# First channel-mixing block in chunks of 1024 tokens, with products of 512 columns and four accumulator banks

## Chip, cores and metric

The kernel runs on one NeuronCore of a Trainium2 chip. The metric is the device time of one execution in microseconds (us); shorter is better.

## The reference

Three blocks follow one another, all in float32. A Fourier block (`rfft` along the sequence, a complex 256 x 256 product, a soft threshold, `irfft`) makes 4 x 3072 tokens of 256 features. The first channel-mixing block follows and is the place of the change; the second one ends the program:

```python
h = x @ w_in                    # 12288 x 256 by 256 x 2048
x = (h - np.tanh(h)) @ w_out    # 2048 x 256

xk = mu_k * x + (1.0 - mu_k) * x_prev
xr = mu_r * x + (1.0 - mu_r) * x_prev
k = np.maximum(xk @ w_k, 0.0)   # 256 x 1024
v = k * k @ w_v                 # 1024 x 256
out = sigmoid(xr @ w_r) * v
```

## The kernel before

Every float32 operand of a product is split in two parts of type float32r, `h` (a copy that rounds, on ScalarE) and `l` (the rest, subtracted on VectorE). One float32 product is then three matmuls, weights `h` by data `h`, `l` by `h` and `h` by `l`, accumulated in one bank of PSUM.

The program has three stages. Stage 1 is the Fourier block (to about 340 us in the profile), which leaves its tokens in DRAM (`ydr`). Stage 2 is the first channel-mixing block. It takes the tokens in 24 chunks of 512 (`chunks`, `CK` = 512). Stage 3, from about 1390 us, is the second block, in chunks of 512 too.

In stage 2, `reg_t` loads a chunk (`yr`) and `token_forms` makes seven forms of it, 256 columns each, for a fast 2 x 2 block product: three blocks of the chunk (B11, B21, B22) and four sums and differences (T1 to T4, made in `yt4`). They are converted to `yh` and `yl`; even chunks have theirs in the pool `pw`, odd chunks in `q1`, so that there are two sets. The weights `w_in` have seven such forms as well (`ah`, `al`).

`reg_pair(c, f2)` is one pass of a chunk over an eighth of the hidden features, and calls `reg_h`. That makes seven products of 256 columns (21 matmuls): one in a bank `g`, two one behind the other in a second bank `g`, and four one behind the other in a bank `m` (tag `y` or `a` in turn). Between two products in a bank its sum is read: from `g` by a copy on ScalarE (`copy`, L819), from `m` by an add on VectorE (`add`, L822), the last one by a copy on ScalarE (L847). Then come tanh (L862), the subtraction (L863), the split in `gh` and `gl` (L345, L348), and 12 matmuls of 512 columns with `w_out`, which add to two accumulator banks `v`. The accumulators are emptied after the eighth pass (L885, L886).

No engine's order is written by hand. Every operation is registered with a priority and an assumed duration, and `_Plan.run` lists the operations in the order in which they would start: of those whose inputs and tiles are free, an engine takes the one with the lowest priority number. On the chip each engine then works through its list in that order, and waits where the list says. A tile of a tag with n buffers can be made anew when all users of the tile n places before it are done.

Of the kernel before, what the change touches and what calls it, by code (L numbers as in the profile page):

```python
# [148 lines left out]
class _Plan:  # L149
# [6 lines left out]
    def op(self, eng, dur, emit, prio, writes=(), reads=(), after=(), lat=SEM, seq=True, nbytes=0):  # L156
# [6 lines left out]
        o.creates, o.frees = [], []  # L163
        for t in reads:
            deps.update(t.writers)
            t.readers.append(o)
        for t in writes:
# [9 lines left out]
            deps.update(r for r in t.readers if r is not o)  # L177
# [134 lines left out]
def fourier_moe_kernel(tc, x, w_r, w_i, b_r, b_i, w_in, w_out, mu_k, mu_r, w_k, w_v, w_rr, c_f, c_e, c_t, c_b, out, nb=B, ydump=None):  # L312
# [291 lines left out]
    def reg_conv(i):  # L604
# [23 lines left out]
        dma("pool" if i < EARLY else "sp", load, pr, [raw[0]], [], 524288, after=[qt[divmod(RAW0 + i * RAW1 // 4, NU)].writers[0] if i < EARLY else yload[int(K["l0"] + K["l1"] * (i - EARLY))]])  # L628
# [79 lines left out]
    def tt(o, a, b, alu, n, prio, writes, reads, **kw):  # L708
        op("dve", c_dve(n), lambda: dve.tensor_tensor(out=o(), in0=a(), in1=b(), op=alu), prio, writes, reads, **kw)
# [5 lines left out]

    def reg_weight(pool_, i, prio):
        st = stage(i, prio)
        h = tile_(pool_, [128, 512], F32R, f"wh{i}")
        l = tile_(pool_, [128, 512], F32R, f"wl{i}")
        hi(whole(h), whole(st), 512, prio)  # L720
        lo(whole(l), whole(st), whole(h), 512, prio)
        return h, l
# [39 lines left out]
    def token_forms(y, t, h, l, pr):
        def yb(d, k):
            return lambda: y()[:, d, k * HK:k * HK + HK]

        def tb(i):
            return lambda: t()[:, i]

        tt(tb(0), yb(0, 1), yb(0, 0), ALU.subtract, HK, pr, [t], [y])
        tt(tb(2), yb(1, 1), yb(0, 1), ALU.subtract, HK, pr, [t], [y], seq=False)  # L770
        tt(tb(1), yb(1, 1), tb(0), ALU.subtract, HK, pr, [t], [y])
        tt(tb(3), yb(1, 0), tb(1), ALU.subtract, HK, pr, [t], [y])
        for o, n, st, src in ((0, 1, y, lambda: y()[:, 0:1, 0:HK]), (1, 2, y, lambda: y()[:, 1].rearrange("p (k c) -> p k c", k=2)), (3, 4, t, t)):
            oc = lambda r, o=o, n=n: r[:, o:o + n]
            hi(cut(h[0], lambda r, oc=oc: oc(h[1](r))), (st, src), n * HK, pr)
            lo(cut(l[0], lambda r, oc=oc: oc(l[1](r))), (st, src), cut(h[0], lambda r, oc=oc: oc(h[1](r))), n * HK, pr)

    def same(r):
        return r

    def reg_t(c):
        b, j = chunks[c]
        pr = P2 + 8 * c - K["t"]
# [5 lines left out]
        c0 = j * CK  # L789
        deps = [ydr[b][k] for k in range(c0 // CH, (c0 + CK - 1) // CH + 1)]  # L790
        dma("sp", lambda: sp.dma_start(out=y(), in_=ydr_t[b][:, :, c0:c0 + CK]), pr - 8, [y], deps, 524288)
        yload.append(plan.ops[-1])

        token_forms(y, t, (h, same), (l, same), pr)
        tv[c] = (h, l)
# [4 lines left out]
    A11, A12, A22, S1, S2, S3, S4 = range(7)  # L800
    B11, B21, B22, T1, T2, T3, T4 = range(7)

    def reg_h(tokens, view, weights, ai, z0, tag):
        yh, yl = tokens
        ah, al = weights

        def product(o, a, t, prio, first):
            def e():
                w, wl_ = ah()[:, a, ai], al()[:, a, ai]
                v, vl = view[0](yh())[:, t], view[1](yl())[:, t]  # L810
                d = o()[:, 0:HK]
                mm(d, w, v, first, False, skip_group_check=True)
                mm(d, wl_, v, False, False, skip_group_check=True)
                mm(d, w, vl, False, True, skip_group_check=True)

            op("pe", 3 * 119, e, prio, [o], [ah, al, yh, yl])

        def copy(o, p, prio):
            op("act", c_act(HK, True), lambda: act.activation(out=o(), in_=p()[:, 0:HK], func=ACTF.Copy), prio, [o], [p])  # L819

        def add(t, half, p, s, prio):
            op("dve", c_dve(HK), lambda: dve.tensor_tensor(out=t()[:, half * HK:half * HK + HK], in0=p()[:, 0:HK], in1=s(), op=ALU.add), prio, [t], [p, s], seq=False)  # L822

        s2 = bank("g")
        p2 = tile_(q1, [128, HK], F32, "p2", 2)
# [3 lines left out]
        p5 = tile_(q1, [128, HK], F32, "p5", 2)  # L829
        p3 = tile_(q1, [128, HK], F32, "p3", 2)  # L830
# [5 lines left out]
        h0 = tile_(q1, [128, CK], F32, "hs0", 2)  # L836
        h1 = tile_(q1, [128, CK], F32, "hs1", 2)
        product(m, A11, B11, z0, True)
        add(h0, 0, m, p2, z0)
        product(m, S2, T2, z0, False)  # L840
        add(h0, 1, m, p3, z0)
        product(m, S3, T3, z0, False)
        add(h1, 1, m, p5, z0)
        product(m, A22, T4, z0, False)

        def last(func):
            op("act", c_act(HK, True), lambda: act.activation(out=h1()[:, 0:HK], in_=m()[:, 0:HK], func=func), z0, [h1], [m], seq=False)  # L847

        return h0, h1, m, last

    def reg_pair(c, f2):
        z0 = P2 + 8 * c + f2
        ai = f2 % 2

        h0, h1, m, last = reg_h(tv[c], (same, same), win[f2 // 2], ai, z0, 'ya'[f2 % 2] if c else 'y')
        last(ACTF.Copy)
        gg = []
        for hs in (h0, h1):
            th = tile_(q1, [128, CK], F32, "th", 2)
            gh = tile_(q1, [128, CK], F32R, "gh2", 3)  # L860
            gl = tile_(q1, [128, CK], F32R, "gl2", 3)
            op("act", c_act(CK, False), lambda th=th, hs=hs: act.activation(out=th(), in_=hs(), func=ACTF.Tanh), z0, [th], [hs])  # L862
            op("dve", c_dve(CK), lambda th=th, hs=hs: dve.tensor_tensor(out=hs(), in0=hs(), in1=th(), op=ALU.subtract), z0, [hs], [th])  # L863
            hi(whole(gh), whole(hs), CK, z0)
            lo(whole(gl), whole(hs), whole(gh), CK, z0)
# [5 lines left out]
        for k in range(2):  # L871
            gh, gl = gg[k]

            def e(k=k, gh=gh, gl=gl):
                for e_ in range(2):
                    s = slice(k * 256 + e_ * 128, k * 256 + e_ * 128 + 128)
                    mm(x2[e_](), wh_()[:, s], gh(), f2 == 0 and k == 0, False)
                    mm(x2[e_](), wl_()[:, s], gh(), False, False)
                    mm(x2[e_](), wh_()[:, s], gl(), False, f2 == 7 and k == 1)

            op("pe", 6 * 232, e, z0 + K["out"], x2, [gh, gl, wh_, wl_])
        if f2 == 7:
            b, j = chunks[c]
            t = tile_(q3, [128, 2, CK], F32, "x2", 2)
            op("act", c_act(CK, True), lambda: act.activation(out=t()[:, 0], in_=x2[0](), func=ACTF.Copy), z0 + K["x2"], [t], [x2[0]])  # L885
            op("act", c_act(CK, True), lambda: act.activation(out=t()[:, 1], in_=x2[1](), func=ACTF.Copy), z0 + K["x2"], [t], [x2[1]], seq=False)  # L886
            dma("sp", lambda: sp.dma_start(out=xdr_t[b][:, :, j * CK:j * CK + CK], in_=t()), z0 + K["x2"], [xdr[b, j]], [t], 524288)

    for c in range(len(chunks)):
# [3 lines left out]
    for c in range(len(chunks) - 1):  # L893
# [6 lines left out]
    wk = [reg_forms(q3, "k", 16, P3 - 30)]  # L900
    wt[24] = [(w, w) for w in reg_weight(q3, 24, P3 - 28)]
    wk.append(reg_forms(pw, "0", 18, P3 - K["kb"]))
    reuse = {1: None, 2: None}
    for i in (20, 21, 22, 23):
        k = 1 if i < 23 else 2
        if reuse[k] is None:
            reuse[k] = [tile_((None, pw, q1)[k], [128, 7, 2, 128], F32R, f"{nm}{k}") for nm in ("ah", "al")]
        st = stage(i, P3 - 10 + (i - 20))
        o = 512 * (i - 20) if k == 1 else 0
# [171 lines left out]
```

## Time and profile before

| | |
|---|---|
| runs | 1955.05, 1955.5, 1957.66 us (median 1955.5) |
| profiled execution | span of 1957.4 us from first to last instruction; no other time is listed for it |
| busy | TensorE (PE) 99%, VectorE (DVE) 81%, ScalarE (ACT) 75% |
| matmuls | 13760 |

The span of the profiled execution lies 1.9 us above the median of the runs and within their extent. PE is the engine of the matmuls, PEld that of their weight loads, DVE is VectorE and ACT is ScalarE. "Busy" of PE covers matmuls that overlap in its pipeline, so it says that PE never ran dry, not how fast it went; how fast is seen from the number of matmuls in a stretch.

### The profile page before, as it was taken

What the parts mean: (1) busy time and instruction counts of PE and PEld (TensorE: products, weight loads), DVE (VectorE), ACT (ScalarE), POOL (GpSimd) and SP (SyncE); (2) the same over time, 40 slices, a digit from 0 to 9 for tenths busy, and PEclk for the clock granted to TensorE, in tenths of its full rate; (3) what the DMA queues carried; (4) which work ended last, traced back from release to release, by engine and by line L of the source; (5) the groups of instructions that cost most, each with busy time, mean ns of one, the idle gap of its engine ahead of it and who ended that gap; (6) DMA issues with size and microseconds to landing.
All of it is one profiled execution on the core that took longest, in us unless ns stands there. A gap on an engine that the chain in (4) does not pass through costs nothing.

```text
span 1957.4 us, 36599 instructions
## 1 busy us (share of the span) xinstructions
PE 1936.6 (99%) x13760; PEld 1815.5 (93%) x13760; DVE 1580.3 (81%) x3057; ACT 1462.8 (75%) x3166; POOL 24.2 (1%) x51
## 2 busy tenths in 40 slices
PE   7999999999999999999999999999999999999998
PEld 5999999998989889998888899888999999999998
DVE  1797878688787888877888887779988888888885
ACT  3765757777777777777777787778877777777774
POOL 2000000000000000000000000000000000000000
PEclk8999999999999999999999999999999999999999
DMA  9989787411010101100111110001111111111101
GB/s 277 292 267 314 254 287 231 141 39 57 28 39 24 49 33 39 39 22 23 38 44 37 46 55 22 22 12 46 50 48 48 48 48 48 48 48 48 48 23 33
DMA packets 96193, 162.37 MB, mean 83 GB/s; under 512 B 11510, under 2 KB 56675, under 8 KB 96016
## 3 DMA queue, kind: packets, MB, share of 16 engines
q1 hardware_dynamic: 90656, 142.66, 23.4%
q0 software_dynamic: 4112, 13.93, 2.4%
q10 hardware_dynamic: 1248, 3.44, 0.5%
q8 instruction: 108, 1.77, 0.4%
q14 instruction: 69, 0.57, 0.1%
HBM read 90.52 MB, written 69.47 MB: 82 GB/s over the span
## 4 chain that ended last, share of the span: by engine, by line
PE 97%; DMA 2%; ACT 1%; SPq 0%; DVE 0%; issue 0%; ACTq 0%
PE v L319 43%; PE y L319 21%; PE g L319 18%; PE a L319 15%; DMA x<-in_x_dram 1%; SPq L477 0%; DMA yr<-ydr 0%; DMA adr<-at 0%; ACT at L466 0%; ACT p L819 0%; DVE ob L1032 0%; ACTq L470 0%; ACTq L1040 0%; DVE xb L348 0%; ACT gh L345 0%
## 5 line engine op out<-in xcount | busy, mean ns | idle before, releaser
L345 ACT ACTIVATE gh<-hs 128x512 fp32r<-128x512 f32 x504 | 318.5, 632 | 134.9 <-PE v L319 124.0
L819 ACT ACTIVATE p<-g 128x256 f32<-128x256 f32 x864 | 318.7, 381 | 83.7 <-PE g L319 66.0
L348 DVE TENSOR_TENSOR gl<-hs,gh 128x512 fp32r<-128x512 f32 x504 | 345.4, 685 | 28.4 <-ACT gh L345 25.2
L863 DVE TENSOR_TENSOR hs<-hs,th 128x512 f32<-128x512 f32 x384 | 261.2, 688 | 94.6 <-ACT th L862 86.9
L822 DVE TENSOR_TENSOR hs<-y,p 128x256 f32<-128x256 f32 x588 | 244.3, 421 | 96.1 <-PE y L319 87.2
L319 PE MATMUL v<-gh,wl 128*128 128x512 f32 x768 | 303.8, 396 | 0.0
L319 PE MATMUL v<-gh,wh 128*128 128x512 f32 x768 | 302.4, 394 | 0.0
L319 PE MATMUL v<-gl,wh 128*128 128x512 f32 x768 | 302.3, 394 | 0.0
L862 ACT ACTIVATE th<-hs 128x512 f32<-128x512 f32 x384 | 238.2, 628 | 19.8 <-DVE hs L822 18.1
L319 PE MATMUL v<-ah,gh 128*128 128x256 f32 x768 | 217.3, 283 | 0.0
L319 PE MATMUL v<-al,gh 128*128 128x256 f32 x768 | 217.3, 283 | 0.0
L319 PE MATMUL v<-ah,gl 128*128 128x256 f32 x768 | 217.3, 283 | 0.0
L319 PE MATMUL g<-yh,ah 128*128 128x256 f32 x648 | 184.8, 285 | 1.4 <-ACT p L819 1.4
L319 PE MATMUL g<-yl,ah 128*128 128x256 f32 x648 | 182.8, 282 | 0.0
L319 PE MATMUL g<-yh,al 128*128 128x256 f32 x648 | 182.8, 282 | 0.0
L319 PEld LDWEIGHTS v<-gl,wh 128*128 128x128 f32 x768 | 144.3, 188 | 33.0
L319 PEld LDWEIGHTS v<-gh,wh 128*128 128x128 f32 x768 | 145.2, 189 | 20.0
L319 PEld LDWEIGHTS v<-gh,wl 128*128 128x128 f32 x768 | 144.8, 188 | 18.8
L319 PEld LDWEIGHTS v<-al,gh 128*128 128x128 f32 x768 | 147.5, 192 | 0.0
L319 PEld LDWEIGHTS v<-ah,gl 128*128 128x128 f32 x768 | 147.5, 192 | 0.0
L319 PEld LDWEIGHTS v<-ah,gh 128*128 128x128 f32 x768 | 147.5, 192 | 0.0
L319 PE MATMUL y<-yh,ah 128*128 128x256 f32 x496 | 140.7, 284 | 0.4 <-DVE hs L822 0.4
(182 smaller groups left out, 4856.7 us busy)
## 6 DMA issues: line engine op xcount, KB each, us to landing
x<-in_x_dram SPq DMA_DIRECT2D x32, 384.0 KB, 6.6
q<-adr SPq DMA_DIRECT2D x48, 256.0 KB, 6.7
vdr<-v SPq DMA_DIRECT2D x48, 256.0 KB, 4.7
vp<-vdr SPq DMA_DIRECT2D x32, 384.0 KB, 6.9
ydr<-yt SPq DMA_DIRECT2D x64, 192.0 KB, 4.7
yr<-ydr SPq DMA_DIRECT2D x24, 512.0 KB, 4.0
xdr<-x SPq DMA_DIRECT2D x24, 512.0 KB, 3.1
xs<-xdr SPq DMA_DIRECT2D x20, 608.0 KB, 4.3
```

Source lines behind the costliest of these rows:

```text
L319: pe.matmul(out=o, lhsT=l, rhs=r, start=st, stop=en, **kw)
L345: op("act", c_act(n, psum), lambda: act.activation(out=o[1](), in_=i[1](), func=ACTF.Copy), prio, [o[0]], [i[0]])
L348: op("dve", c_dve(n), lambda: dve.tensor_tensor(out=o[1](), in0=i[1](), in1=h[1]().bitcast(F32), op=ALU.subtract), prio, [o[0]], [i[0], h[0]])
L819: op("act", c_act(HK, True), lambda: act.activation(out=o(), in_=p()[:, 0:HK], func=ACTF.Copy), prio, [o], [p])
L822: op("dve", c_dve(HK), lambda: dve.tensor_tensor(out=t()[:, half * HK:half * HK + HK], in0=p()[:, 0:HK], in1=s(), op=ALU.add), prio, [t], ...
L862: op("act", c_act(CK, False), lambda th=th, hs=hs: act.activation(out=th(), in_=hs(), func=ACTF.Tanh), z0, [th], [hs])
L863: op("dve", c_dve(CK), lambda th=th, hs=hs: dve.tensor_tensor(out=hs(), in0=hs(), in1=th(), op=ALU.subtract), z0, [hs], [th])
```

## The change

Stage 2 now works on 13 spans in place of 24 chunks: one chunk alone, 11 spans of two chunks (1024 tokens), one chunk alone (`spans`). In a span of two the products are 512 columns wide, so that one matmul does what two did; the copies and adds are 512 wide, and tanh, subtraction and split 1024 wide. The four products in bank `m` always use tag `y` (two banks), since a span has four accumulators, two with tag `v` and two with tag `a`. The token forms have one set of tiles (`fb`, `fc` in `pw`, `ft` in `q3`) in place of two; `homes` says which form lies where. The partial copies share one ring of five (`pp`), the sums one of four (`hs`), `gh` and `gl` have two buffers of 1024 columns in place of three of 512. Weights are placed in other pools: `w_k` now takes the tiles of the first half of `w_in` (`wk` at P3 - 4 and P3 - 1, before: one in a tile of its own at P3 - 30), `w_v` and `w_r` those of the second half, and in stage 3 the gates, the loaded tokens and the outputs use tiles of stage 2. Stage 1's operations, and the counts and sizes of stage 3's, stay.

The core of the diff:

```diff
+    spans = [(0, 1)] + [(i, 2) for i in range(1, len(chunks) - 1, 2)] + [(len(chunks) - 1, 1)]
...
     def reg_t(c):
-        own = pw if c % 2 == 0 else q1
-        y = tile_(pw, [128, 2, CK], F32, "yr", 1)
-        t = tile_(pw, [128, 4, HK], F32, "yt4", 1)
-        h = tile_(own, [128, 7, HK], F32R, "yh", 1)
-        l = tile_(own, [128, 7, HK], F32R, "yl", 1)
+        i0, k = spans[c]
+        n = k * HK
+        y = tile_(pw, [128, 2, 1024], F32, "yr", 1)
+        t = tile_(pw, [128, 2048], F32, "yt4", 1)
...
+        tv[c] = token_forms(y, lambda: y()[:, :, 0:2 * n], t, n, homes("ft" if k == 2 else "e"), pr)
...
+    def homes(kind):
+        def pair(pool_, n, tag):
+            return [tile_(pool_, [128, n], F32R, tag + x, 1) for x in "hl"]
...
+        f1, f2, ft = pair(pw, 768, "fb"), pair(pw, 1024, "fc"), pair(q3, 2048, "ft")
+        return {B11: (f1, 0), B21: (f2, 0), B22: (f2, 1), T1: (ft, 0), T2: (ft, 1), T3: (ft, 2), T4: (ft, 3)}
...
     def product(o, a, t, prio, first):
-                d = o()[:, 0:HK]
-                mm(d, w, v, first, False, skip_group_check=True)
+                d = o()[:, 0:n]
+                mm(d, w, v(), first, False, skip_group_check=True)
...
     def reg_pair(c, f2):
-        h0, h1, m, last = reg_h(tv[c], (same, same), win[f2 // 2], ai, z0, 'ya'[f2 % 2] if c else 'y')
+        i0, k2 = spans[c]
+        one, _, last = reg_h(k2 * HK, tv[c], win[f2 // 2], f2 % 2, z0, "y")
...
-        for hs in (h0, h1):
-            th = tile_(q1, [128, CK], F32, "th", 2)
-            gh = tile_(q1, [128, CK], F32R, "gh2", 3)
-            gl = tile_(q1, [128, CK], F32R, "gl2", 3)
+        for hs in one:
+            th = tile_(q1, [128, 1024], F32, "th", 2)
+            gh = tile_(q1, [128, 1024], F32R, "gh", 2)
+            gl = tile_(q1, [128, 1024], F32R, "gl", 2)
...
-            xa[c] = [bank("v") for _ in range(2)]
+            xa[c] = [[bank("va"[g]) for _ in range(2)] for g in range(k2)]
...
-    wk = [reg_forms(q3, "k", 16, P3 - 30)]
-    wk.append(reg_forms(pw, "0", 18, P3 - K["kb"]))
+    wk = [reg_forms(pw, "0", 16, P3 - 4), reg_forms(pw, "1", 18, P3 - 1)]
```

How the lists of two engines change where the prediction looks. First PE in the middle of stage 2, before. The names are output bank, then data, then weights; `g` and `y`, `a` are the banks of the products.

```order
L319 MATMUL a<-yh,ah_3836 128x256 [waits DVE_49]
L319 MATMUL a<-yh,al_3941 128x256
L319 MATMUL a<-yl,ah_3836 128x256
L319 MATMUL g<-yh,ah_4087 128x256 [waits Activation_49]
L319 MATMUL g<-yh,al_4098 128x256
L319 MATMUL g<-yl,ah_4087 128x256
L319 MATMUL g<-yh,ah_4087 128x256 [waits Activation_49]
L319 MATMUL g<-yh,al_4098 128x256
L319 MATMUL g<-yl,ah_4087 128x256
```

The same place in the changed kernel: the last matmul of a product in bank `g`, a product in bank `y`, six matmuls with `w_out` (`wo`) into the accumulators `a`, and the next product in the same bank `y`.

```order
L327 MATMUL g<-fcl,ah_4216 128x512
L327 MATMUL y<-fth,ah_4216 128x512 [waits DVE_49]
L327 MATMUL y<-fth,al_4231 128x512
L327 MATMUL y<-ftl,ah_4216 128x512
L327 MATMUL a<-gh,wo_4368 128x512 x2
L327 MATMUL a<-gl,wo_4368 128x512
L327 MATMUL a<-gh,wo_4368 128x512 x2
L327 MATMUL a<-gl,wo_4368 128x512
L327 MATMUL y<-fth,ah_4216 128x512 [waits DVE_49]
```

Three products of 256 became one of 512, and between two products in one bank `y` there are six matmuls, during which VectorE has to read the bank.

Second, ACT where the tokens of the next chunk are converted, before (`yh`; `yr` is the loaded chunk).

```order
L345 ACTIVATE yh<-yr 128x256 [waits DMAHW4_49]
...
L345 ACTIVATE yh<-yr 128x512
...
L345 ACTIVATE yh<-yt_7154 128x1024
```

The same in the changed kernel, at the end of a span (`fbh`, `fch`, `fth` are the tiles of the forms, `yr` and `yt` what they are made from).

```order
L830 ACTIVATE fbh<-yr 128x512 [waits DMAHW1_49,PE_49]
L830 ACTIVATE fch<-yr 128x1024 [waits DMAHW2_49,PE_49]
L877 ACTIVATE pp<-g 128x512 [waits PE_49]
L353 ACTIVATE gh<-hs 128x1024 [waits PE_49]
L922 ACTIVATE th<-hs 128x1024 [waits DVE_49]
L353 ACTIVATE gh<-hs 128x1024 [waits PE_49]
L830 ACTIVATE fth<-yt_8731 128x1024 [waits PE_49]
L908 ACTIVATE hs<-y 128x512 [waits PE_49]
L830 ACTIVATE fth<-yt_8731 128x1024
L922 ACTIVATE th<-hs 128x1024 [waits DVE_49,Activation_49]
L877 ACTIVATE pp<-g 128x512 [waits PE_49]
```

The conversions before waited for the load alone; now each waits for PE, which must be through with the span before.

## Rows read from the trace of the kernel before

**Rows 1.** The page, busy time and share of the span, PE.

```profile
PE 1936.6 (99%) x13760; PEld 1815.5 (93%) x13760; DVE 1580.3 (81%) x3057; ACT 1462.8 (75%) x3166; POOL 24.2 (1%) x51
```

**Rows 2.** The page, chain that ended last, by engine.

```profile
PE 97%; DMA 2%; ACT 1%; SPq 0%; DVE 0%; issue 0%; ACTq 0%
```

**Rows 3.** Busy time by stretch: stages 2, 3 and their two borders (x: instructions).

```profile
core 0: us, PE busy (x) PEld busy (x) DVE busy (x) ACT busy (x) POOL busy (x), PEclk, DMA share, GB/s
400.00:1300.00 900.00, 900.00 (x5621) 809.98 (x5620) 730.44 (x1411) 686.04 (x1475) 0.00 (x0) 1.00 0.11 36
1400.00:1900.00 500.00, 500.00 (x4169) 500.00 (x4169) 436.32 (x865) 399.25 (x880) 0.00 (x0) 1.00 0.17 46
300.00:400.00 100.00, 98.65 (x743) 93.75 (x743) 77.80 (x156) 75.77 (x167) 0.00 (x0) 1.00 0.56 177
1300.00:1400.00 100.00, 99.38 (x672) 91.47 (x671) 88.29 (x170) 85.55 (x185) 0.00 (x0) 1.00 0.14 41
```

**Rows 4.** Timeline of PE, two runs of twelve 512-column matmuls (start, us, instruction).

```profile
683.66 0.39 PE L319 MATMUL v<-gh,wh 128*128 128x512 f32 x1
...
686.45 0.28 PE L319 MATMUL y<-yh,ah 128*128 128x256 f32 x1
...
694.28 0.40 PE L319 MATMUL v<-gh,wh 128*128 128x512 f32 x1
...
695.66 0.39 PE L319 MATMUL v<-gh,wh 128*128 128x512 f32 x1
...
697.02 0.28 PE L319 MATMUL a<-yh,ah 128*128 128x256 f32 x1
```

**Rows 5.** Waits of PE, 290 to 1950 us (total, times, longest).

```profile
PE g L319 <- ACT p L819: 1.4, 1, 1.4
PE y L319 <- DVE hs L822: 0.4, 1, 0.4
PE a L319 <- ACT sg L1031: 0.3, 1, 0.3
```

**Rows 6.** Groups of ACT and DVE instructions (busy, mean ns | idle before).

```profile
L819 ACT ACTIVATE p<-g 128x256 f32<-128x256 f32 x864 | 318.7, 381 | 83.7 <-PE g L319 66.0 <-DVE hs L822 14.9
L862 ACT ACTIVATE th<-hs 128x512 f32<-128x512 f32 x384 | 238.2, 628 | 19.8 <-DVE hs L822 18.1
L885 ACT ACTIVATE x<-v 128x512 f32<-128x512 f32 x24 | 14.3, 596 | 6.8 <-PE v L319 6.8
L345 ACT ACTIVATE yh<-yt 128x1024 fp32r<-128x1024 f32 x36 | 37.9, 1051 | 0.0
L863 DVE TENSOR_TENSOR hs<-hs,th 128x512 f32<-128x512 f32 x384 | 261.2, 688 | 94.6 <-ACT th L862 86.9
L822 DVE TENSOR_TENSOR hs<-y,p 128x256 f32<-128x256 f32 x588 | 244.3, 421 | 96.1 <-PE y L319 87.2 <-ACT hs L847 1.4 <-ACT p L819 1.4
L348 DVE TENSOR_TENSOR yl<-yt,yh 128x1024 fp32r<-128x1024 f32 x36 | 43.9, 1220 | 2.2 <-ACT yh L345 1.0
L536 DVE TENSOR_TENSOR t<-y,bias 128x512 f32<-128x512 f32 x44 | 30.2, 687 | 22.5 <-PE y L319 19.8 <-DMA bias<-in_b_i_dram 2.2
```

**Rows 7.** Timeline, an add on VectorE behind the matmul that it waited for.

```profile
700.80 0.28 PE L319 MATMUL a<-yl,ah 128*128 128x256 f32 x1
...
701.16 0.28 PE L319 MATMUL y<-yl,ah 128*128 128x256 f32 x1
...
701.55 0.42 DVE L822 TENSOR_TENSOR hs<-y,p 128x256 f32<-128x256 f32 x1 [1.44 <-PE y L319]
```

**Rows 8.** DMA issues between 355 and 375 us (count, KB, us to landing).

```profile
ydr<-yt SPq DMA_DIRECT2D x10, 192.0 KB, 2.6
```

More of the change, by code (lines that the diff above doesn't have):

```diff
@@ L154, in __init__, with op @@
         self.rings = {}
-    def op(self, eng, dur, emit, prio, writes=(), reads=(), after=(), lat=SEM, seq=True, nbytes=0):
+    def op(self, eng, dur, emit, prio, writes=(), reads=(), after=(), lat=SEM, seq=True, nbytes=0, war=True):
         o = _Op()
@@ L163, in op @@
         o.creates, o.frees = [], []
+        whole_reads = []
         for t in reads:
-            deps.update(t.writers)
+            if isinstance(t, tuple):
+                t, parts = t
+                deps.update(parts)
+            else:
+                deps.update(t.writers)
             t.readers.append(o)
+            whole_reads.append(t)
+        reads = whole_reads
         for t in writes:
@@ L176, in op @@
             t.writers.append(o)
-            deps.update(r for r in t.readers if r is not o)
+            if war:
+                deps.update(r for r in t.readers if r is not o)
         for t in list(reads) + list(writes):
@@ L749, in reg_forms, with reg_plain @@
         return h, l
+    def reg_plain(pool_, tag, loads):
+        ws = [tile_(pool_, [128, 7, 2, 128], F32R, nm + tag) for nm in ("ah", "al")]
+        got = []
+        for n, (i, prio) in enumerate(loads):
+            st = stage(i, prio)
+            hc, lc = (cut(w, lambda r, o=512 * n: r.rearrange("p s a c -> p (s a c)")[:, o:o + 512]) for w in ws)
+            hi(hc, whole(st), 512, prio)
+            lo(lc, whole(st), hc, 512, prio)
+            got.append((hc, lc))
+        return got
+    WIN = (pw, pw, q2, q2)
+    WOUT = (pw, q1, q1, q2, q2, q2, q3, q3)
     win = {}
@@ L773, in token_forms @@
[L773 to L779, printed above, removed]
[L781 to L791 removed]
+            return lambda: t()[:, i * n:i * n + n]
@@ new lines, in token_forms @@
+        return got
+    def reg_t(c):
+        i0, k = spans[c]
+        n = k * HK
+        pr = P2 + 8 * i0 - K["t"]
+        y = tile_(pw, [128, 2, 1024], F32, "yr", 1)
+        t = tile_(pw, [128, 2048], F32, "yt4", 1)
+        for g in range(k):
+            b, j = chunks[i0 + g]
+            c0 = j * CK
+            deps = [ydr[b][x] for x in range(c0 // CH, (c0 + CK - 1) // CH + 1)]
+            dma("sp", lambda b=b, c0=c0, g=g: sp.dma_start(out=y()[:, :, g * CK:g * CK + CK], in_=ydr_t[b][:, :, c0:c0 + CK]), pr - 8, [y], deps, 524288)
@@ L792, in reg_t, with reg_h @@
         yload.append(plan.ops[-1])
-        token_forms(y, t, (h, same), (l, same), pr)
-        tv[c] = (h, l)
+        tv[c] = token_forms(y, lambda: y()[:, :, 0:2 * n], t, n, homes("ft" if k == 2 else "e"), pr)
     xa = {}
     xdr = {k: _Tile(dram, None, None, None, 1, fixed=True) for k in chunks}
[L800 to L804, printed above, removed]
+    def reg_h(n, forms, weights, ai, z0, tag):
@@ L805, in reg_h, with at_ @@
         ah, al = weights
+        wide = n == CK
+        one = [tile_(q1, [128, 1024], F32, "hs", 4) for _ in range(2 if wide else 1)]
+        made = {}
+        def at_(f, half):
+            o = half * n if wide else f * CK + half * n
+            return one[f if wide else 0], lambda: one[f if wide else 0]()[:, o:o + n]
         def product(o, a, t, prio, first):
+            (vr, v), (vlr, vl) = forms[t]
             def e():
                 w, wl_ = ah()[:, a, ai], al()[:, a, ai]
-                v, vl = view[0](yh())[:, t], view[1](yl())[:, t]
@@ new lines, in e, with add @@
+                mm(d, w, v(), first, False, skip_group_check=True)
+                mm(d, wl_, v(), False, False, skip_group_check=True)
+                mm(d, w, vl(), False, True, skip_group_check=True)
+            op("pe", 3 * (228 if wide else 119), e, prio, [o], [ah, al, vr, vlr])
+        def copy(o, p, prio):
+            op("act", c_act(n, True), lambda: act.activation(out=o()[:, 0:n], in_=p()[:, 0:n], func=ACTF.Copy), prio, [o], [p])
+        def add(f, half, p, s, prio):
+            t, v = at_(f, half)
+            made[f, half] = op("dve", c_dve(n), lambda: dve.tensor_tensor(out=v(), in0=p()[:, 0:n], in1=s()[:, 0:n], op=ALU.add), prio, [t], [p, s], seq=False)
@@ L890, in fourier_moe_kernel @@
+    for c in range(NS):
         reg_t(c)
@@ L892, in fourier_moe_kernel @@
         reg_conv(i)
-    for c in range(len(chunks) - 1):
+    for c in range(NS - 1):
         for f2 in range(8):
```

277 lines of the change are left out of this document (152 added, 125 removed).

## The prediction

> **What bounds the kernel now.** I read the page's busy times first. TensorE is busy for 99% of the span, VectorE for 81%, ScalarE for 75% [rows 1]. The chain that ended last says the same of the path: 97% of it is TensorE [rows 2]. So the question is what the change does to TensorE's own work, and whether it opens gaps in it.
>
> Busy time can't tell how fast TensorE goes, so I took the stretches next and divided time by matmuls. In stage 3, where all matmuls have 256 columns, 500 us hold 4169 [rows 3]. About two of them only reach in from an edge, which leaves 500 / 4167 = 0.1200 us each. In stage 2, 900 us hold 5621, so 900 / 5619 = 0.1602 us each [rows 3]. A pass of stage 2 is 21 matmuls of 256 columns and 12 of 512: 33 x 0.1602 = 5.286 us. With 0.1200 for each of the 21, 2.766 us are left for the 12, or **0.2305 us for a matmul of 512 columns**. Two of 256 cost 0.2400. The clock was granted in full in both stages (1.00, the level of 2.4 GHz) [rows 3].
>
> The timeline gives the spread of the 0.2305. One run of twelve takes 686.45 - 683.66 = 2.79 us, 0.2325 each; another takes 697.02 - 694.28 = 2.74 us, 0.2283 each, and its last six 1.36 us, 0.2267 each [rows 4].
>
> TensorE waits almost never between 290 and 1950 us: three waits, 2.1 us in all, at the borders of the stages [rows 5]. The stretches around the borders miss 1.35 us and 0.62 us of busy time [rows 3]. There is nothing else to win there.
>
> **The change, part by part.** *Products.* 22 of the 24 chunks are paired. They had 22 x 8 x 21 = 3696 matmuls of 256 columns; they get 1848 of 512. On TensorE, which is the path, that is 3696 x 0.1200 - 1848 x 0.2305 = 443.5 - 426.0 = **17.6 us less**. The matmuls with `w_out` stay as they are, 24 in a pass of a span.
>
> The bounds: after the change all 45 matmuls of such a pass have 512 columns, 3960 in the 88 passes, and I know only runs of at most twelve. At 0.2267 the 3960 would take 3960 x 0.0038 = 15.0 us less than at 0.2305, 32.6 us in all; at 0.2283 it is 8.7 less, 26.3 in all; at 0.2325 it is 7.9 more, and 9.7 us are left of the gain. I take 0.2305, since it comes from some 2040 such matmuls (5619 x 12 / 33) and the others from twelve each.
>
> The Trainium skill's page "TensorE: Matmul & The Clock Gate", under "Back-to-back issue gap", gives a matmul N / 2.4 ns and a fixed 2.5 ns. By that, two of 256 columns cost 2.5 ns more than one of 512, and the 1848 pairs would give an estimated 4.6 us. The rows differ: 0.1200 us for 256 columns lie 13 ns above 256 / 2.4, so there is more to save than the page has.
>
> *ScalarE and VectorE.* A pass of a span (45 x 0.2305 = 10.37 us) gives VectorE three adds of 512 from PSUM (0.687, as the addition of the bias), two subtractions and two splits of 1024 (1.220, as the split of `yt`): 6.9 us. ScalarE has four reads of 512 from PSUM (0.596) and four operations of 1024 (1.051): 6.6 us [rows 6]. Both fit under 10.37 us, and both shrink: two passes before had, on VectorE, six adds at 0.421, four subtractions at 0.688 and four splits like them, 8.0 us [rows 6]. The token forms come to under 1 us a pass on either. So they cost nothing, covered by TensorE; how their waits fall is the third rival's business.
>
> *Three products in a bank, with a read between.* Before, a product was three matmuls of 256 columns and tags `y` and `a` gave four banks. Now `y` alone gives two. In the list of the changed kernel six matmuls stand between two products in one bank `y`. An add began 0.39 us after the start of the last matmul that it waited for (701.16 to 701.55) [rows 7]. A matmul of 512 columns lasts 0.11 us longer (0.39 against 0.28) [rows 4, 7]. So the next product could go on 0.50 + 0.69 + about 0.11 for the hand-over back, 1.30 us after that start. TensorE comes to it after 7 x 0.2305 = 1.61 us. The cover is 0.31 us with VectorE free, and I book nothing. Without the cover, up to 0.9 us of a 1.220 us operation in the way would show, once a pass.
>
> *One set of token forms.* Before, a chunk's forms went to the set that was not in use. Now the conversion on ScalarE waits for the last product of the span before, and the next span's products wait for it and for the split on VectorE: 1.051 + 1.220 us and three hand-overs, about 2.7 us [rows 6]. In the list 18 matmuls stand between the last product that reads T1 to T4 (`ft`) and the first that reads them anew, 4.15 us. Cover 1.4 us, booked at nothing. If it goes, each further operation of 1024 in the way costs about 1.1 us at each of 12 borders of spans.
>
> *Start of stage 2.* `ft` lies where stage 1's last stores come from, and ScalarE, in its list, waits for their landing: 2.6 us there [rows 8]. Between the last copy of stage 1 that it waits for and this wait stand a copy of 384, two reads of 256, a tanh of 1024 and two splits of 512, over 2.6 us by [rows 6]. Nothing.
>
> *End of stage 2.* The first half of `w_k` (four additions and three splits of 256 columns at about 0.42, one split of 1024 at 1.220: 4.2 us of VectorE [rows 6]) and `w_r` (0.69) moved from 30 steps ahead into the last span. Between 1300 and 1400 us VectorE was busy for 88.3 of 100 us [rows 3], so 11.7 us were free and 6.8 are left. From both sides: 2.0 us better, if the present gaps close, to 4.9 us worse, if all of it lies on the path. I take **1.5 us worse**, the side of the crowded engine but far from its end, since room is left.
>
> *DMA.* Each chunk is still loaded and stored once, and the engines' share is 0.11 in stage 2 [rows 3]: nothing.
>
> Sum: -17.6 + 1.5 = **-16.1 us**. Against the profiled execution that is 1957.4 - 16.1 = 1941.3 us of span; against the median of 1955.5, 1.9 us below that span, 1939.5 us after rounding.
>
> **The rivals.** *First, TensorE at its best rate.* All matmuls alike, as in the last six of the second row of twelve: 0.2267, so -32.6 + 1.5, about 1924.5 us of time. For it: the first few after a change of width take longer. Against: the first row of twelve never gets there [rows 4].
>
> *Second, width buys little.* No row shows a product of 512 columns with these operands; it could cost nearly the 0.2400 us of two of 256. Half-way to that from the first row of twelve (0.2325) is 0.2363, so 1848 x 0.0037 = 6.8 us are saved, and with 1.5 us lost it is about 1950 us. Against: both runs of twelve lie below 0.2363 [rows 4]. The page's rule above would land near here.
>
> *Third, the borders.* The one set of forms, and the late weights, cost about 1 us at each of 12 borders: 11 us, about 1950.5 us. For it: ScalarE's list puts tanh, splits and copies between the conversions there. Against: the cover of 1.4 us.
>
> *Fourth, and slower, the add in VectorE's queue.* The add between two products waits behind an operation that is now 1.220 us long, and TensorE waits with it. It decides from 17.6 / 88 = 0.20 us a pass, where the gain is gone; past 0.24 us it is slower by over 0.2%. If the add met VectorE at random, operations of 1024 would be running for 4.9 of 10.37 us, and one in three adds would overrun the cover, by 0.45 us on average: 0.16 us a pass, 14 us. At 0.35 us a pass it is 31 us, about 1970 us. For it: before, four banks and adds of 0.421 us left more room. Against: TensorE has no such wait in 900 us of stage 2, with VectorE 81% busy there [rows 3, 5], and VectorE's load falls.
>
> That the products do not become wide is excluded, since the list holds 1848 matmuls fewer.
>
> **How the numbers follow.** Forecast 0.66; best rate 0.06; little width 0.06; borders 0.10; the add 0.12. The predicted time is the forecast's, 1939.5 us. Its own range, from the rates 0.2283 and 0.2325 and the ends of the last border, is about 1927 to 1951 us. The borders and the little width lie at its upper end, and 2 us for what else they could cost together make it 1927 to 1953 us; left out are the best rate and the rival that is slower, 0.18. About 0.2%, 3.9 us, is what a measurement of this kernel can tell from no change. Faster by more: forecast, best rate and, as they lie near this bound, two thirds of the second and third rivals, 0.82. Slower by more: nearly all of the add's, 0.11. Within: the rest, 0.07.
>
> **What would show it.** Right: 88 passes of about 10.4 us, so 434 matmuls or so in 100 us in the middle of stage 2, TensorE at 100% there, and VectorE near 75%. The first and second rivals show in that count (441 and 429). The third shows as waits of `g` for the conversions, ten alike, the fourth as waits of `y` for the add, 88 or more. A change in the pace of stages 1 or 3 would make the whole reckoning wrong.

## The result, and the profile after

| | before | after |
|---|---|---|
| median, us | 1956.58 | 1932.82 (1930.27 to 1936.34) |
| ratio to before, 95% interval | | 0.9871, 0.9842 to 0.99 |
| span of the profiled execution, us | 1957.4 | 1929.4 |

The change is faster by some 24 us in the medians and by 28.0 us in the two profiled spans. 16.1 us were forecast. Three series of it, each beside the kernel before on one chip, gave 0.9871 (0.9842 to 0.99), 0.9872 (0.9854 to 0.989) and 0.9855 (0.9838 to 0.9872).

The page after, with the busy times [rows 1] and the chain that ended last [rows 2]:

```profile
PE 1907.7 (99%) x11912; PEld 1724.2 (89%) x11912; DVE 1507.8 (78%) x2345; ACT 1352.0 (70%) x2410; POOL 24.1 (1%) x51
...
PE 95%; DMA 2%; DVE 1%; ACT 1%; issue 0%; SPq 0%; DVEq 0%; POOL 0%; ACTq 0%
```

TensorE is still the path. The busy times by stretch [rows 3]:

```profile
core 0: us, PE busy (x) PEld busy (x) DVE busy (x) ACT busy (x) POOL busy (x), PEclk, DMA share, GB/s
400.00:1200.00 800.00, 800.00 (x3530) 662.13 (x3529) 618.51 (x697) 540.62 (x706) 0.00 (x0) 1.00 0.10 35
1400.00:1800.00 400.00, 400.00 (x3335) 400.00 (x3334) 344.37 (x688) 317.27 (x707) 0.00 (x0) 1.00 0.18 48
300.00:400.00 100.00, 98.11 (x668) 91.42 (x667) 67.52 (x112) 66.25 (x129) 0.00 (x0) 0.95 0.57 174
1300.00:1400.00 100.00, 97.95 (x723) 93.17 (x722) 95.88 (x181) 88.06 (x185) 0.00 (x0) 1.00 0.21 63
```

In the middle 800 us hold 3530 matmuls, all of 512 columns. Two reach in from the edge, so one takes 800 / 3528 = **0.2268 us**. Stage 3 is unchanged (400 / 3333 = 0.1200). The two borders are worse: from 300 to 400 us TensorE is busy 0.5 us less than before and its granted clock reads 0.95; from 1300 to 1400 us it is busy 1.4 us less, and VectorE 95.88 us instead of 88.29.

The timeline of TensorE in the middle has no pattern left [rows 4]; from the first of these rows to the last it is 16 matmuls in 3.63 us, 0.2269 each, products and `w_out` alike:

```profile
902.18 0.39 PE L327 MATMUL g<-fth,ah 128*128 128x512 f32 x1
...
903.54 0.62 PE L327 MATMUL v<-gh,wo 128*128 128x512 f32 x2
...
904.90 0.39 PE L327 MATMUL y<-fth,ah 128*128 128x512 f32 x1
...
905.81 0.39 PE L327 MATMUL g<-fch,al 128*128 128x512 f32 x1
```

TensorE's waits from 290 to 1950 us [rows 5] add up to 4.2 us, against 2.1 before. All lie at the borders and at the end:

```profile
PE a L327 <- ACT yt L587: 1.5, 2, 0.9
PE y L327 <- DVE hs L881: 1.2, 3, 0.6
PE a L327 <- ACT wo L1094: 1.0, 1, 1.0
PE v L327 <- DVE ws L1095: 0.5, 1, 0.5
```

The first wait is new. ScalarE's timeline at the border of the first two stages shows what stood ahead of the copies (`yt<-a`) that empty TensorE's bank `a` (in brackets: idle time before, and who ended it):

```profile
310.62 0.48 ACT L587 ACTIVATE yt<-a 128x384 f32<-128x384 f32 x1
314.01 0.63 ACT L353 ACTIVATE wo<-ws 128x512 fp32r<-128x512 f32 x1 [2.91 <-PE y L327]
...
316.07 0.86 ACT L587 ACTIVATE yt<-a 128x384 f32<-128x384 f32 x2
```

The split of a `w_out` tile (`wo`) waited 2.91 us at the head of ScalarE's queue, until the last product of stage 1 (`y`) was through. The change has moved tiles 1 and 2 of `w_out` from `pw` to `q1`, whose space that product still reads. TensorE's timeline, and the clock granted to it, in the next microseconds:

```profile
313.81 1.92 PE L327 MATMUL a<-e_sb,vp 96*128 96x96 f32 x16
316.60 5.72 PE L327 MATMUL a<-e_sb,vp 96*128 96x96 f32 x32 [0.86 <-ACT yt L587]
```

```profile
314.00:318.00 4.00, 3.14 (x28) 2.97 (x28) 2.98 (x6) 3.15 (x7) 0.00 (x0) 1.00 0.92 271
318.00:320.00 2.00, 2.00 (x13) 2.00 (x12) 0.65 (x2) 1.27 (x3) 0.00 (x0) 0.55 0.83 252
326.00:328.00 2.00, 2.00 (x11) 2.00 (x11) 0.00 (x0) 0.90 (x2) 0.00 (x0) 0.50 1.07 304
328.00:330.00 2.00, 2.00 (x17) 2.00 (x17) 1.72 (x5) 2.00 (x7) 0.00 (x0) 0.89 1.00 335
```

TensorE waits 0.86 us, and from 318 to 328 us it works at 0.50, the level of 1.2 GHz. What that cost can be read from a second profile of the change (it comes up again in the next section), which has the same matmuls in the same order and the same wait, but a granted clock of 1.00 behind it. From the end of the wait to the first product of stage 2, first here, then there:

```profile
328.14 0.41 PE L327 MATMUL g<-fch,ah 128*128 128x256 f32 x1
```

```profile
321.31 3.81 PE L327 MATMUL a<-e_sb,vp 96*128 96x96 f32 x32 [0.86 <-ACT yt L587]
...
328.19 0.28 PE L327 MATMUL g<-fch,ah 128*128 128x256 f32 x1
```

That is 328.14 - 316.60 = 11.54 us against 328.19 - 321.31 = 6.88 us: the low clock lost 4.7 us, over five times what the wait itself took.

### The profile page after: what moved, and what is told of

Read it like the earlier page. It is cut to its first block, busy times and chain, and to the rows that moved or that the text cites. A ratio compares the mean times of both kernels' runs of the same rounds, so it can differ in the third digit from the quotient of the medians.

```text
span 1929.4 us, 31048 instructions
## 1 busy us (share of the span) xinstructions
PE 1907.7 (99%) x11912; PEld 1724.2 (89%) x11912; DVE 1507.8 (78%) x2345; ACT 1352.0 (70%) x2410; POOL 24.1 (1%) x51
## 4 chain that ended last, share of the span: by engine, by line
PE 95%; DMA 2%; DVE 1%; ACT 1%; issue 0%; SPq 0%; DVEq 0%; POOL 0%; ACTq 0%
PE v L327 30%; PE y L327 27%; PE a L327 21%; PE g L327 17%; DMA x<-in_x_dram 1%; DMA v<-in_w_r_dram 0%; DMA vp<-vdr 0%; DMA q<-adr 0%; DMA adr<-at 0%; SPq L485 0%; DVE hs L881 0%; ACT th L922 0%; DMA ws<-wdr 0%; ACT at L474 0%; DVE al L356 0%
## 5 line engine op out<-in xcount | busy, mean ns | idle before, releaser
L881 DVE TENSOR_TENSOR hs<-y,pp 128x256 f32<-128x256 f32 (+1 forms) x600 | 319.3, 539 | 159.5 <-PE y L327 127.0
L877 ACT ACTIVATE pp<-g 128x256 f32<-128x256 f32 (+1 forms) x600 | 275.3, 474 | 118.5 <-PE g L327 112.3
L923 DVE TENSOR_TENSOR hs<-hs,th 128x1024 f32<-128x1024 f32 x192 | 234.7, 1223 | 73.1 <-ACT th L922 69.8
L353 ACT ACTIVATE gh<-hs 128x1024 fp32r<-128x1024 f32 x192 | 202.7, 1056 | 111.3 <-PE a L327 103.6
L356 DVE TENSOR_TENSOR gl<-hs,gh 128x1024 fp32r<-128x1024 f32 x192 | 234.7, 1222 | 54.1 <-ACT gh L353 52.0
L327 PE MATMUL v<-gh,wo 128*128 128x512 f32 x832 | 256.8, 390 | 0.0
L922 ACT ACTIVATE th<-hs 128x1024 f32<-128x1024 f32 x192 | 201.9, 1057 | 74.7 <-DVE hs L881 73.7
L327 PE MATMUL a<-gh,wo 128*128 128x512 f32 x704 | 216.9, 389 | 0.0
L327 PE MATMUL v<-gl,wo 128*128 128x512 f32 x416 | 161.9, 389 | 0.0
L327 PE MATMUL y<-fth,ah 128*128 128x512 f32 (+1 forms) x456 | 157.1, 344 | 0.0
```

What stands on the lines that cost most here:

```text
L327: pe.matmul(out=o, lhsT=l, rhs=r, start=st, stop=en, **kw)
L353: op("act", c_act(n, psum), lambda: act.activation(out=o[1](), in_=i[1](), func=ACTF.Copy), prio, [o[0]], [i[0]])
L356: op("dve", c_dve(n), lambda: dve.tensor_tensor(out=o[1](), in0=i[1](), in1=h[1]().bitcast(F32), op=ALU.subtract), prio, [o[0]], [i[0], h[0]])
L877: op("act", c_act(n, True), lambda: act.activation(out=o()[:, 0:n], in_=p()[:, 0:n], func=ACTF.Copy), prio, [o], [p])
L881: made[f, half] = op("dve", c_dve(n), lambda: dve.tensor_tensor(out=v(), in0=p()[:, 0:n], in1=s()[:, 0:n], op=ALU.add), prio, [t], [p, s], ...
L922: op("act", c_act(1024, False), lambda th=th, hs=hs: act.activation(out=th(), in_=hs(), func=ACTF.Tanh), z0, [th], [hs])
```

## The experiments

**The middle: width or layout?** All matmuls of the middle got faster, those of `w_out` too, which the change leaves at 512 columns. Either 512 columns run slower among 256-column matmuls (my theory), or the new place of the tiles matters, or both. The first run brings the mix of widths back and keeps the new tiles:

```diff
-                d = o()[:, 0:n]
-                mm(d, w, v(), first, False, skip_group_check=True)
...
+                for s in range(0, n, HK):
+                    d, r, rl = o()[:, s:s + HK], v()[:, s:s + HK], vl()[:, s:s + HK]
+                    mm(d, w, r, first and s == 0, False, skip_group_check=True)
...
```

> In the 1024-token chunks each product of 512 columns goes as two of 256 with the same weights into the halves of the same bank; tiles, the order of all other instructions and the 1024-wide operations stay. Theory (a 512-wide matmul is slower where widths alternate, whatever the tiles are): the 3,696 products take 0.119 to 0.120 us each and the 2,112 of w_out go back from 0.2267 to 0.231 to 0.232 us; together 31 to 35 us over the change, 1964 to 1968 us. Rival (the new layout of the tiles is what made w_out's matmuls fast): w_out stays at 0.2267 us, and only 3,696 x 0.1200 - 1,848 x 0.2267 = +24.6 us come, 1957 us. Second rival (the wide operations of VectorE and ScalarE or the fewer tiles were the gain): under +5 us.

The change ran beside it on the same chip:

> The changed kernel as it is, beside the others on the same chip. Expected by both theories: a median near 1932.8 us, 440 to 443 512-wide matmuls in 100 us between 400 and 1200 us. What it is to tell: in the profile of the change ScalarE's split of w_out tile 1 holds its queue for 2.9 us at 311 us, TensorE then waits 0.86 us at 316 us and its granted clock reads 0.50 from 318 to 328 us. If that fall follows from the wait, it is there again in this profile, at the same place (theory); if it is chance, this profile has it elsewhere or not at all, and the span is about 5 us shorter (rival).

The change took 1934.54 us, 0.9872 (0.9854 to 0.989) of the kernel before. With halved products it was 1960.91 us, 1.0014 (1.0005 to 1.0022): **26.4 us more**, the gain gone. The stretch, and two pieces of the timeline, of the halved products:

```profile
400.00:1200.00 800.00, 800.00 (x5017) 723.79 (x5016) 602.23 (x678) 525.28 (x684) 0.00 (x0) 1.00 0.10 35
```

```profile
903.05 0.63 PE L327 MATMUL v<-gh,wo 128*128 128x512 f32 x2
...
904.44 0.28 PE L327 MATMUL y<-fth,ah 128*128 128x256 f32 x1
...
917.07 0.63 PE L327 MATMUL v<-gh,wo 128*128 128x512 f32 x2
...
918.46 0.61 PE L327 MATMUL a<-gh,wo 128*128 128x512 f32 x2
...
919.82 0.28 PE L327 MATMUL y<-fth,ah 128*128 128x256 f32 x1
```

800 / 5015 = 0.1595 us for each of 66 matmuls of a pass; 42 at 0.1200 leave 5.49 us for the 24 of `w_out`, 0.2287 each. Six of them in the timeline take 1.39 us, 0.2317 each. So `w_out` slows down again with nothing but the width of its neighbours changed, but by 0.0019 us of the 0.0037 us that part it from the kernel before (0.2305), and the total lies between theory and rival. The second piece is a run of twelve: its first six take 1.39 us, its last six 1.36 us, 0.2267 each, the rate of the pure stream. By the start times in the trace all 67 runs of twelve between 400 and 1200 us do the same (0.2312, then 0.2267). In the kernel before, the last six go at 0.2267 in 18 of 37 such runs and at 0.2325 in the other 19. So the matmuls right behind a change of width are slow in both kernels, but the kernel before has a second slowness further on, which the mix of widths did not bring back. That the time is the same as before is in part chance: the middle is still a little faster (66 x 0.1595 us a pass, against 66 x 0.1602 for two passes before), and the losses at the borders are still there. VectorE and ScalarE have their wide operations in this run, and none of the gain: the second rival is out. Next a middle of one width again, the narrow one; `w_out`'s matmuls are halved too:

```diff
+                    for h_ in range(0, CK, HK):
+                        d = x2[g][e_]()[:, h_:h_ + HK]
+                        v, vl = gh()[:, o + h_:o + h_ + HK], gl()[:, o + h_:o + h_ + HK]
...
```

> As the run with halved products, and w_out's matmuls of the 1024-token chunks go as two of 256 columns as well, so that the middle of the kernel has one width again, the narrow one. Theory (each matmul costs its columns and about 13 ns, and a stream of one width runs clean): 7,920 matmuls at 0.1200 us instead of 3,960 at 0.2267 us, +52.7 us, 1985 us, 833 in 100 us between 400 and 1200 us. Rival (halves that follow each other with tiles laid out anew run faster than 0.120 us, as after a change of width in the kernel before, 0.113 to 0.118 us): +15 to +45 us. Second rival (halving brings waits of its own): over +60 us with TensorE below 99% there.

```profile
600.00:1200.00 600.00, 600.00 (x5002) 600.00 (x5001) 438.29 (x491) 383.71 (x502) 0.00 (x0) 1.00 0.10 35
```

1987.43 us, 52.9 us over the change; 600 / 5000 = 0.1200 us each, the theory's rate. (Its total of +52.7 us came closer than these medians can tell, since single executions of the change lie up to 11 us apart.) In streams of one width 256 columns more cost 0.2268 - 0.1200 = 0.1068 us, and every matmul 13 ns besides (2 x 0.1200 - 0.2268). Then the other side, the kernel before with one piece of the new layout:

```diff
-        h = tile_(pool_, [128, 512], F32R, f"wh{i}")
-        l = tile_(pool_, [128, 512], F32R, f"wl{i}")
...
+        w = tile_(pool_, [128, 1024], F32R, f"wo{i}")
+        hc, lc = cut(w, lambda r: r[:, 0:512]), cut(w, lambda r: r[:, 512:1024])
...
```

> The kernel before with one part of the change: the high and low half of each w_out tile lie side by side in one tile of 1024, pools and all instructions otherwise as they were. Theory (the 512-wide matmuls of the kernel before are slow because 256-wide ones stand between them): they stay at 0.232 us from start to start, the time within 2 us of the kernel before. Rival (the layout of the tiles sets their rate): they come to 0.2267 to 0.229 us, 2,304 x 0.003 to 0.0055 us = -7 to -13 us.

```profile
400.00:1300.00 900.00, 900.00 (x5628) 810.76 (x5627) 730.37 (x1409) 686.40 (x1476) 0.00 (x0) 1.00 0.11 36
```

1957.99 us, 1.0002 (0.9994 to 1.0011) of the kernel before. Seven more matmuls than before fit into 900 us, 0.1%; reckoned as in the prediction, `w_out` takes 0.2299 us. That layout makes little of it: the slower kind of the last six of a run of twelve goes at 0.2300 us instead of 0.2325, in 19 of 37 runs as before. What else slows `w_out` in the kernel before (0.2305 against 0.2287 with halved products) was not tried and stays open; the other changes of place and the somewhat shorter runs of one width there are candidates.

**Is the other engines' work hidden?** First the wide operations cut in two again:

```diff
-            op("act", c_act(1024, False), lambda th=th, hs=hs: act.activation(out=th(), in_=hs(), func=ACTF.Tanh), z0, [th], [hs])
...
+            for r in (slice(0, CK), slice(CK, 1024)):
+                op("act", c_act(CK, False), lambda th=th, hs=hs, r=r: act.activation(out=th()[:, r], in_=hs()[:, r], func=ACTF.Tanh), z0, [th], [hs], seq=False)
...
```

> The change with its four 1024-wide operations per hidden tile (tanh, subtraction, high part, low part) cut into two of 512 each; matmuls and tiles stay. By the groups of the two profiles (1.056 against 2 x 0.630 us on ScalarE, 1.222 against 2 x 0.687 us on VectorE) ScalarE gets 78 us and VectorE 58 us more to do, 8 and 6 points of their share in the middle. Theory (the gain is TensorE's, the width of these operations is hidden behind it): TensorE stays at 100% and 442 or 443 matmuls in 100 us from 500 to 1200 us, 0.98 to 0.99 of the kernel before, as the change. Rival (the wide operations carry part of the gain by making tiles ready sooner): TensorE waits in the middle, over 10 us of the 26 us are gone.

```profile
600.00:1200.00 600.00, 600.00 (x2642) 494.40 (x2641) 470.00 (x747) 423.53 (x761) 0.00 (x0) 1.00 0.10 35
```

1937.07 us, 0.9894 (0.9879 to 0.9909); the change has 0.9872 (0.9854 to 0.989). In these 600 us the change itself has 2649 matmuls, 7 more: 1.6 us, over the 900 us of the middle 2.4 us. The width of these operations is hidden but for that. Then the fourth rival, the add in VectorE's queue, with one more operation in that queue:

```diff
+            if hs is one[0]:
+                op("dve", 1, lambda gl=gl, hs=hs, gh=gh: dve.tensor_tensor(out=gl(), in0=hs(), in1=gh().bitcast(F32), op=ALU.subtract), z0, [gl], [hs, gh])
```

> The change with one more 1024-wide subtraction on VectorE in each pass (the low part of the first hidden tile written a second time): about 1.2 us per pass of 10.2 us, so VectorE goes from 75 to about 87% in the middle, and every add of a product that stands behind it in VectorE's queue comes up to 1.2 us later. Theory (the passes are covered: nothing waits on an add until VectorE is full): TensorE stays at 100%, at most +2 us. Rival (the prediction's case of the add in VectorE's queue: the next product in the same bank is only six matmuls behind): TensorE waits for sums of VectorE, and from 0.2 us in each of 96 passes on it costs +19 us or more.

```profile
600.00:1200.00 600.00, 594.49 (x2602) 485.48 (x2601) 512.47 (x564) 396.74 (x520) 0.00 (x0) 1.00 0.10 35
...
1300.00:1400.00 100.00, 92.71 (x586) 81.44 (x584) 88.78 (x147) 76.56 (x151) 0.00 (x0) 0.97 0.18 55
```

```profile
PE y L327 <- DVE hs L881: 14.0, 21, 1.6
```

1963.76 us, 1.0029 (1.0019 to 1.0039): the whole gain is gone. The rival's mechanism is real, with VectorE at only 85%: TensorE waits for the add, 14.0 us in all in the list of waits. In the middle 47 matmuls are missing in 600 us, 10.7 us or 0.18 us in each of 59 passes, of 1.22 us more work for VectorE; some 1.0 us a pass was absorbed. At the end of stage 2 it is 5.2 us in one stretch of 100. So I halved the added work (`[:, 0:CK]` on all three operands):

> As the run with the doubled subtraction, which cost some 26 us over the change, but only half of the columns are written a second time: about 0.7 us of VectorE in each pass instead of 1.2 us. Theory (there is slack of 0.9 us or so per pass, 1.2 less the 0.27 us that each of 96 passes lost): the delay fits into it, TensorE stays at 442 matmuls or more in 100 us, at most +3 us over the change. Rival (no slack: the loss goes with the delay): 0.7 / 1.2 of the 26 us, +15 us.

```profile
600.00:1200.00 600.00, 600.00 (x2642) 494.32 (x2641) 492.43 (x574) 402.95 (x527) 0.00 (x0) 1.00 0.10 35
...
1300.00:1400.00 100.00, 94.54 (x639) 85.81 (x638) 91.48 (x168) 83.61 (x170) 0.00 (x0) 0.98 0.19 60
```

The theory was right for the middle and wrong for the total. In the middle 7 matmuls are missing, 0.03 us a pass. But the time is 1943.75 us, 0.9929 (0.9916 to 0.9942), and the change beside it 0.9855 (0.9838 to 0.9872): 14 us more. By the profiles most of it lies at the borders: 97.95 - 94.54 = 3.4 us from 1300 to 1400 us, where the change already keeps VectorE busy for 95.88 us, and a fall of the clock (0.66 from 320 to 340 us), which the change beside it did not have.

**The border of the first two stages.** One line of the planner makes the splits of `w_out` tiles 1 and 2 count the end of the product whose space they take, not its start:

```diff
-                        t = o.start + 1e-3
+                        t = o.end + o.lat if x.creates and x.creates[0].tag in ("wo1", "wo2") else o.start + 1e-3
```

> The change with one line of the planner altered: it counts that the first tiles of the pool whose space the first stage's last products still read (w_out tiles 1 and 2) come free when those products end, not when they start, and so puts their splits behind other work of ScalarE. Theory (the split held ScalarE's queue, TensorE waited 0.86 us for the copy behind it and its granted clock then fell to half for 10 us): the wait and the fall go, 0.9 + 5 us, to 1926 to 1928 us, and the granted clock reads 1.00 from 300 to 400 us. Rival (the fall comes of the narrow 96-column matmuls there, wait or no wait): about -1 us, and the clock still reads 0.50 for some 10 us.

```profile
300.00:400.00 100.00, 98.21 (x710) 91.55 (x709) 72.66 (x122) 70.24 (x136) 0.00 (x0) 1.00 0.57 183
```

1930.63 us, 0.9855 (0.9839 to 0.9872), against 1934.54 us for the change on the same chip: 3.9 us better in the medians, with intervals that overlap; 0.9 + 5 us were expected. The 0.86 us wait and the low clock are gone, the stretch holds 710 matmuls instead of 668, but a wait of 1.2 us for a copy (`pp`) has come. Was the fall due to the 0.86 us wait? The second profile of the change says that the wait alone does not bring it. The same wait is there, without a fall; the clock fell some 16 us later, after a wait of 1.8 us for `pp`, which stood behind a split that waited for its load:

```profile
334.44 0.63 ACT L353 ACTIVATE wo<-ws 128x512 fp32r<-128x512 f32 x1 [2.26 <-DMA ws<-wdr]
```

```profile
332.00:336.00 4.00, 2.18 (x17) 1.98 (x18) 2.01 (x6) 1.39 (x4) 0.00 (x0) 1.00 1.03 296
336.00:340.00 4.00, 3.80 (x20) 3.18 (x19) 4.00 (x8) 3.64 (x8) 0.00 (x0) 0.71 1.01 339
340.00:344.00 4.00, 4.00 (x20) 4.00 (x20) 3.36 (x5) 1.27 (x2) 0.00 (x0) 0.50 0.99 320
```

So I took the splits further back, by letting the planner count every load of weights 3 us later:

```diff
-                o.lat = line + 950.0 - o.end
+                o.lat = line + 950.0 - o.end + (3000 if o.creates and o.creates[0].tag == "ws" else 0)
```

> The run with the later split, with one more number in the planner: a weight tile loaded from memory counts as 3 us later than before, so the splits of weights that ScalarE does stand behind the copies that TensorE waits for at the border of the first and second stage, where the transfers run at 280 to 370 GB/s. Theory (what is left of the waits at that border are splits that wait for their load with copies queued behind them; the granted clock falls after such a wait): TensorE's waits from 300 to 400 us fall under 0.5 us in sum, the granted clock stays at 1.00 there, 1924 to 1927 us, under the changed kernel in every execution. Rival (the splits now come too late for the first passes): new waits for the weights, 1930 us or more.

It gave 1930.6 us, 0.986 (0.9847 to 0.9874), the rival's time and not the theory's. The granted clock stayed at 1.00 at that border, but TensorE's waits from 300 to 400 us add up to 1.3 us instead of under 0.5; the longest, 0.9, is for an add of VectorE. Then once more, with the change beside it:

> The version with the two altered numbers of the planner, beside the change on the same chip. Theory (without the splits ahead of the copies the clock does not fall at the border): 2 to 5 us under the change, no execution over 1932 us. Rival (the same time in other waits): within 1 us of the change.

> The changed kernel once more, beside the next run. Theory (a wait of TensorE at the border of the first and second stage is followed in most executions by some 10 us at half the clock): median 1932 to 1935 us, single executions from 1925 to 1937 us. Rival (the fall was an accident of the executions so far): 1926 to 1929 us.

1929.35 us (0.9848, 0.9834 to 0.9861) against 1929.9 us for the change (0.9855, 0.9838 to 0.9872): the same within the error, and the expected 2 to 5 us are missed. The change's own median lies between the two expectations for it. The rows say why. First the later loads, then the third profile of the change, which has the 0.86 us wait (0.9 in its list) and no fall of the clock at all:

```profile
300.00:400.00 100.00, 98.54 (x709) 92.05 (x708) 76.40 (x127) 73.25 (x139) 0.00 (x0) 1.00 0.57 182
```

```profile
300.00:400.00 100.00, 97.36 (x692) 89.96 (x691) 71.19 (x118) 68.41 (x134) 0.00 (x0) 1.00 0.58 177
```

What is shown: eight profiles have the change's border (three of the change, halved products, all halves, narrow operations, both longer subtractions); in six the clock fell there (to 0.66 to 0.94 in the mean of 320 to 340 us), in two it did not. In the three with altered splits and the two with the old border it never did. The eight executions with later loads lie between 1927.9 and 1931.2 us, the fourteen of the change between 1925.5 and 1936.8 us. The executions with later loads scatter less; that they are faster in the median is not shown. What decides whether the clock falls after a wait stays open.

The rows of a fixed place say more than the medians. Up to about 285 us all these programs give each engine the same instructions in the same order. One batch of 16 matmuls ahead of that starts at these times: in the kernel before, in the three profiles of the change, with the later split, and in the two profiles with later loads:

```profile
270.84 1.92 PE L319 MATMUL a<-e_sb,vp 96*128 96x96 f32 x16
268.59 1.92 PE L327 MATMUL a<-e_sb,vp 96*128 96x96 f32 x16
273.30 1.92 PE L327 MATMUL a<-e_sb,vp 96*128 96x96 f32 x16
270.90 1.92 PE L327 MATMUL a<-e_sb,vp 96*128 96x96 f32 x16
273.40 1.92 PE L327 MATMUL a<-e_sb,vp 96*128 96x96 f32 x16
274.18 1.92 PE L327 MATMUL a<-e_sb,vp 96*128 96x96 f32 x16
272.64 1.92 PE L327 MATMUL a<-e_sb,vp 96*128 96x96 f32 x16
```

So executions are up to 5.6 us apart before anything differs between the programs. The spans are 1957.4, 1929.4, 1935.0, 1928.1, 1928.9, 1929.4 and 1927.7 us. What is left of them from that batch on is 1686.6 us before, 1660.8, 1661.7 and 1657.2 us with the change (the last one is the profile without a fall), and 1655.5, 1655.2 and 1655.1 us with altered splits. Behind the batch the altered planner is about 2 us better than the change without a fall, and 5 to 7 us better than with one, close to the 0.9 + 5 us expected. In the medians the scatter of stage 1 covers that.

## Why the prediction was right, and which term was mis-sized

*TensorE is the bound* held: 99% before and after, 95% of the chain.

*Products*, -17.6 us. This is the term that was mis-sized. 0.1200 us for 256 columns was right. **0.2305 us for 512 was a price of the kernel before, with its mix of widths, and not of the width**: in a stream of 512 columns it is 0.2268, and the term is 3696 x 0.1200 - 1848 x 0.2268 = -24.4 us. "The matmuls with `w_out` stay as they are" failed with it: their 2112 lost 0.0037 us each, another -7.8 us. Together -32.2 us, the first rival's -32.6, to which I gave 0.06. By the sign that I had named, the middle was the first rival's: its count of 441 in 100 us came (3528 in 800 us), not the forecast's 434. The experiments show 24.4 us of it as the price of the width in pure streams, and 2112 x 0.0019 = 4.0 us more as the mix; the cause of the other 3.8 us stays open. The row that gave the price was there, the last six of a run of twelve [rows 4]. I preferred the mean of 2040 matmuls to one of six, but all 2040 stood in the same mix, and after the change none does.

The page "TensorE: Matmul & The Clock Gate" of the Trainium skill gives 2.5 ns of fixed cost for a matmul at the full clock, in its formula for the gap of a single one under "Back-to-back issue gap". The measurement differs and decides: 13 ns in the streams of 256 and of 512 columns alike.

*ScalarE and VectorE*, nothing: right, and now with its limits. 0.7 us more of VectorE in a pass costs 0.03 us of it, 1.2 us costs 0.18.

*Three products in a bank*, nothing: right, and the cover of 0.31 us was reckoned about right too. In the changed kernel an add and the next product in its bank stand like this:

```profile
909.24 0.68 DVE L881 TENSOR_TENSOR hs<-y,pp 128x512 f32<-128x512 f32 x1
...
910.34 0.39 PE L327 MATMUL y<-fth,ah 128*128 128x512 f32 x1
```

The product starts 910.34 - 909.92 = 0.42 us after the add ends (0.40 in the median of the trace's 119 such pairs between 400 and 1300 us), of which I had put 0.11 down to the hand-over. That a pass absorbs some 1.0 us of added work is another measure: the added operation need not stand just in front of such an add. How often it does was not counted.

*One set of token forms*, nothing: right; no wait of `g` appears in the list, and the third rival's waits at the borders of the spans are out.

*Start of stage 2*, nothing: wrong. I followed ScalarE's wait for the stores of stage 1. What held it was the split of a tile that the change had moved into space still being read. It cost 0.5 us of TensorE's busy time and, in the profiled execution, 4.7 us by the clock at 0.50.

*End of stage 2*, +1.5 us: measured 99.38 - 97.95 = 1.4 us of busy time [rows 3], with VectorE busy for 96% there.

The new sum is -32.2 + 1.4 + 0.5 + 4.7 = -25.6 us for the profiled execution. Its span fell by 28.0 us, of which 25.8 lie behind the batch at about 270 us (1686.6 to 1660.8) and 2.2 ahead of it, where nothing was changed. So the forecast of 1939.5 us was 6.7 us too high, inside its range: a gain 14.6 us too small in the middle, and 5.2 us of losses at the first border that it did not have. That the two misses point opposite ways is luck: with the middle as measured and the borders as forecast the sum is -32.2 + 1.5, about 1925 us, just below the range of 1927 to 1953.

## What to carry to other kernels

A duration taken from a stretch with several kinds of instructions is a price for that mix; when the change leaves one kind alone, look for rows where that kind already stands alone, even if they are few. Where a tile moves to another pool, ask who still reads that space and what stands behind the first write to it in the writer's queue: there the one wait was short, and the low clock that followed in one profile cost over five times as much. And an engine with a fifth of its time to spare in the middle can have none at a border, so a cover is measured in each stage for itself.

## What the runs showed of the hardware that I had not expected

Matmuls of 512 columns took 0.2268 us among their like, and 0.2287 to 0.2305 us with matmuls of 256 columns between them, at a granted clock of 1.00 and without a wait. With the new tiles the slowdown is over after six matmuls of a run (0.2312, then 0.2267 us); with the old ones the last six of a run of twelve went at 0.2267 us in about half of the runs and at 0.2325 us in the others. TensorE's granted clock fell to 0.50 for some 10 us after a wait of 0.86 us in one profile and of 1.8 us in another, in stretches where it was busy before and after, and fell there in six of eight profiles, while the same 0.86 us wait in another profile, and 1.35 us in the kernel before [rows 3, 5], passed without a fall.
